# A chunked delta rule ahead of a mixture of experts on one core: keys of odd heads stored with the batches swapped

## The chip, the cores and the metric

The kernel runs on one core of a Trainium2 chip. It is one launch that computes everything. The time is the device time of an execution in microseconds; the figure for a kernel is the median of its runs. Five engines work side by side, each through its own queue in order: PE (matmuls, with the weight loads shown apart as PEld), DVE and ACT (elementwise work, both may read PSUM), POOL (elementwise work and indirect DMAs, no access to PSUM) and SP (DMA issues).

## The reference

Keys are normalised, then each head keeps a 48x48 state that every token reads and updates; the answers of all heads, side by side, are the 384 inputs of a router that sends each token to two of eight experts.

```
B, H, S, D = 4, 8, 768, 48        # N = B*S = 3072 tokens, E = 8, F = 1024
k_n = k / (norm(k, axis=-1, keepdims=True) + 1e-06)
for t in range(S):
    y[:, :, t] = einsum('bhd,bhde->bhe', q[:, :, t], state)
    v_old = einsum('bhde,bhd->bhe', state, kt)
    state = state + bt[..., None] * einsum('bhd,bhe->bhde', kt, vt - v_old)
x = y.transpose(0, 2, 1, 3).reshape(B * S, H * D)
noisy = x @ w_gate + log1p(exp(x @ w_noise)) * noise
# the two largest of each token, softmax over them, then
out[mask] += weight * (relu(x[mask] @ w1[e]) @ w2[e])
```

## The kernel before, in words

**Units and steps.** The sequence is cut into 12 chunks of 64 tokens (C = 64). A *unit* is one chunk of two batches, all 8 heads: partitions 0 to 63 hold the 64 tokens of one batch, 64 to 127 those of the other (`rows_of`). There are 2 units for a chunk (NU) and 24 in all; unit n belongs to chunk n // 2. Four units, two chunks, are a *step* (US = 4, six steps). Heads go in NP = 4 pairs j; z or y is the parity of a head within its pair, b the batch within the unit.

**What a unit does**, in the order of the data:

- `load` brings k, q and v of a unit, two DMAs for each (one per batch). SP issues them; ACT issues half of the k loads of the first step.
- `products`: PE turns k (`turned`, L549), ACT copies the turned keys to `kT` (L556), where rows 0 to 63 are the even head of a pair and 64 to 127 the odd one, and columns are the tokens of batch 0, then batch 1. `by_token` (L567) multiplies keys with keys, 32 matmuls of 64x64 over four 64-row tiles of the array. ACT (and DVE in the first step) copy the result to `gd` and `at`.
- Once per step DVE inverts 32x32 triangles of all four units at once: a transpose (L613), lengths of the keys (L641 to L652), 30 columns of two operations (L691, L695), two transposes back (L717, L725). These run at one instruction after another for some 30 us.
- `join` builds the inverse of 64x64 from the 32x32 pieces, with PE (L768, L774) and ACT (L748, L782, L786), into `w64`.
- `within`: PE turns q (L549), multiplies it with the keys (L567), DVE masks the result into `qk` (L810).
- `recur`: POOL scales v (L829); PE reads the old state with the keys (L567 with `st`), DVE subtracts (L848); PE multiplies with the inverse, the *solution* u (L858), ACT copies it (L865); PE sums keys times u (L876, the *state sum*) and DVE adds it to the state (L888, L892); POOL copies the new state into `wide` (L901), where each pair of heads has its two 48x48 states on a block diagonal of 128x96.
- `answer`: PE multiplies q with `wide` (L923, 16 matmuls, the *state answer*) and `qk` with u (L934, 32 matmuls, the *chunk answer*) into the same PSUM tile; ACT copies it to y (L959); PE turns y (L943), ACT copies (L965), PE multiplies with the router's weights (L948), ACT copies the logits (L973).

In the solution and the chunk answer every batch's 64 rows give results for the same 64 rows, so of the four 64-row tiles (row half times column half) they use (0, 0) and (1, 1).

**Routing and experts.** `route` chooses experts for one or two steps and POOL spreads their rows to DRAM by indirect DMA (L383). `early` computes part of expert 0 from rows of the first steps (L1256 to L1319). Everything from `rest` on (L1531 and others) belongs to the other experts and comes after the last step.

**Order.** `Jobs` holds every piece of the attention as a job with an engine, a planned cost and what it reads and writes, plans them greedily in time, and emits them in the planned order; each engine's queue keeps that order on the chip. PSUM is given out by the same plan: two single-bank tiles (`bank(1)`) and three two-bank tiles (`bank(2)`); jobs that may run ahead (`ahead=True`: key products, q-k products, the turns of k and q) use only the first single and the first two pairs. `opens` takes a tile from the plan, `closes` gives it back. Of those free, the one that has been empty longest is taken.

**Buffers.** Rings are indexed by unit: 12 slots for k, 10 for kT, 4 for q, v, qT, qk, and u, 2 per unit of a chunk for states and for `wide`. `early` reuses slots of k, kT and q.

Of the kernel before, what the change touches and what calls it, by code (L numbers as in the profile page):

```python
# [19 lines left out]
C = 64  # L20
DP = 64
# [211 lines left out]
def kernel(  # L233
# [39 lines left out]
    nc = tc.nc  # L273
# [7 lines left out]
    NU = B // 2  # L281
# [148 lines left out]
    def deltanet(ictx):  # L430
# [27 lines left out]
        def per_head(p):  # L458

            return p.tile[:, 0 : H * D].rearrange("p (h d) -> p h d", d=D)  # L460

# [4 lines left out]
        def by_parity(t):  # L466
            return t.rearrange("p (j z) d -> p z j d", z=2)

        NK, NT_, NW = 3 * US, 3 * US - NU, US + NU

        NQ, N_U, N_ST = 2 * NU, 2 * NU, 2
# [5 lines left out]

        wides = [
            ring(
                [128, 2, NP, 2 * D], f"wide{u}_", 2,  # L480
                lambda t: [t[0:DP, :, :, D:], t[DP:, :, :, 0:D]],
            )
            for u in range(NU)
        ]
# [22 lines left out]


# [15 lines left out]
        def load(n, name):  # L524
            c, u = divmod(n, NU)
            src, t, size = {"k": (k, kps, NK), "q": (q, qps, NQ), "v": (v, vs, NQ)}[name]
            for i, rows in enumerate(rows_of):
                engine = ACT if name == "k" and n < US and i else SP
                queue = nc.scalar if engine == ACT else nc.sync
# [9 lines left out]
        def halves(name, slot):  # L539
            return [(name, slot, i) for i in range(2)]  # L540
# [21 lines left out]
        def by_token(out, lhsT, rhs):  # L562

            for j in range(NP):
                for b in range(2):
                    for z in range(2):
                        nc.tensor.matmul(  # L567
                            out[rows_of[b], z, j], lhsT[rows_of[z], j, rows_of[b]],
                            rhs(rows_of[z], j, b), start=(j == 0), stop=(j == NP - 1),
                            skip_group_check=True,  # L570
                        )

        def products(n):
# [10 lines left out]
                    two_banks(p, C), kTs(n), lambda z, j, b: kTs(n)[z, j, rows_of[b]]  # L584
# [212 lines left out]
        def within(n):  # L797
# [6 lines left out]
                    two_banks(p, C), kTs(n), lambda z, j, b: qTs(n)[z, j, rows_of[b]]  # L804
# [12 lines left out]
        def recur(n):  # L817
# [4 lines left out]
            old, new, wide = sts[z](c), sts[z](c + 1), wides[z](c + 1)  # L822
            v_key, u_key = halves("v", n % NQ), ("u", n % N_U)
            every_w = [("w", n % NW), *(("w", n % NW, lo) for lo in range(0, 128, Q))]

# [10 lines left out]
            if c:  # L836
# [4 lines left out]
                        two_banks(p_b, D), kTs(n), lambda r, j, b: old[r, b, j]  # L841
# [11 lines left out]
            p_u = bank(1)  # L853

            def solve():
                for h in range(H):
                    for b in rows_of:
                        nc.tensor.matmul(  # L858
# [1026 lines left out]
```

## Time and profile before

| | |
|---|---|
| runs | 874.31, 875.14, 883.87 us; median 875.14 |
| profiled execution | 875.56 us; span from the first to the last instruction 873.8 us |
| instructions | 21991 |
| busy, share of the span | PE 772.6 us (88%), DVE 570.9 (65%), ACT 333.0 (38%), POOL 385.4 (44%) |
| first and last L613 (an inversion begins) | 17.1 and 228.0 us |
| last L725 (an inversion ends) | 298.2 us, 1.9 long |
| last logits multiplied (L948) | 358.6 us |
| DMA | 93.8 MB, mean 107 GB/s |

The profile is of one execution, taken on the chip; times in it count from the first instruction. Busy time of PE is modelled at the ends of matmuls. A group of instructions is written as line, engine, operation, output <- inputs, tile size of a matmul's stationary operand (rows*columns), shape of the output, count; then its busy time and the mean duration of one in ns, then the idle time of its engine just before and what ended it. "issue" stands for a wait for nothing that the profile shows. The granted PE clock is a share of the full clock: in this kernel it is 1.0 or 0.5 in each stretch of 3.4 us, and 0.89 in the mean.

### The profile page before, as it was taken

To read this page: it belongs to the slowest core of one execution; us is meant where nothing else is said; L and a number is where in the kernel's file an instruction comes from. 1 tells how busy PE (TensorE), PEld (TensorE's weight loads), DVE (VectorE), ACT (ScalarE), POOL (GpSimd) and SP (SyncE) were. 2 spreads that over 40 slices of the span, in tenths; PEclk is the share of its full clock that TensorE was granted. 3 is DMA by queue.
4 is the path that set the end of the run, shared out by engine and by line. 5 is a ranking of instruction groups with operands and counts; after the bars stand their busy time and mean duration, and the time that the engine had idled before them with its cause. 6 is when DMAs were issued, how large, how long until landed. Compare 5 with 4: busy or idle time off the path is not lost.

```text
span 873.8 us, 21991 instructions
## 1 busy us (share of the span) xinstructions
PE 772.6 (88%) x9110; PEld 602.7 (69%) x9110; DVE 570.9 (65%) x1295; ACT 333.0 (38%) x791; POOL 385.4 (44%) x424
## 2 busy tenths in 40 slices
PE   4657878887699786899999999999999999999995
PEld 3446767776588675646757858759668678588594
DVE  5987899989578542201579567677587496685651
ACT  4573667745354171311243053151251340531510
POOL 3021212021552544121268387477676674874511
PEclk8756878975597867899999999999999999999998
DMA  4789634624332313071272342524333421401101
GB/s 69 136 236 246 141 93 128 172 43 128 110 88 65 102 49 129 20 266 52 82 240 82 103 140 84 174 58 150 109 116 107 124 91 37 147 1 58 56 20 42
DMA packets 119087, 93.78 MB, mean 107 GB/s; under 512 B 84646, under 2 KB 109255, under 8 KB 118976
## 3 DMA queue, kind: packets, MB, share of 16 engines
q1 hardware_dynamic: 107312, 64.54, 26.7%
q0 software_dynamic: 9552, 27.33, 9.3%
q8 instruction: 74, 1.21, 0.6%
q10 hardware_dynamic: 2112, 0.39, 0.3%
q14 instruction: 37, 0.30, 0.1%
HBM read 58.82 MB, written 34.81 MB: 107 GB/s over the span
## 4 chain that ended last, share of the span: by engine, by line
PE 69%; issue 10%; DVE 9%; ACT 6%; POOL 3%; DMA 1%; another core or an unknown queue 1%; SPq 0%; POOLq 0%; DVEq 0%; ACTq 0%
PE inner L1531 24%; PE outer L1531 15%; PE pair L567 4%; PE pair L1282 3%; PE pair L1305 3%; PE single L858 3%; PE single L934 3%; DVE part L691 2%; DVE t L695 2%; PE single L549 2%; PE inner L1636 2%; PE inner L1563 2%; PE single L923 2%; PE single L948 1%; PE single L768 1%
## 5 line engine op out<-in xcount | busy, mean ns | idle before, releaser
L1590 DVE TENSOR_TENSOR hT<-hT,inner 128x416 f32<-128x416 f32 x182 | 105.5, 587 | 61.6 <-PE inner L1531 51.6
L1596 ACT ACTIVATE hT<-inner 128x416 f32<-128x416 f32 x112 | 57.9, 517 | 171.3 <-PE inner L1531 169.1
L424 POOL DMA_INDIRECT out_dram<-sums,index x49 | 50.8, 1037 | 113.7 <-DVE sums L1431 105.3
L1531 PE MATMUL inner<-s_x,w1e 128*128 128x416 f32 x196 | 78.7, 512 | 0.0
L1431 DVE SCALAR_TENSOR_TENSOR sums<-outer,gate,sums 128x192 f32<-128x192 f32 x112 | 45.1, 414 | 50.2 <-PE outer L1531 50.2
L901 POOL COPY wide<-st 64x384 f32<-64x384 f32 x44 | 24.8, 564 | 116.4 <-DVE st L888 94.7
L695 DVE TENSOR_TENSOR t<-t,part 128x30 f32<-128x30 f32 (+9 forms) x180 | 66.1, 367 | 6.2
L691 DVE TENSOR_TENSOR part<-t 128x30 f32<-128x30 f32 (+9 forms) x180 | 62.0, 345 | 5.0
L1585 ACT ACTIVATE hT<-hT 128x416 f32<-128x416 f32 x112 | 59.8, 547 | 12.2 <-DVE hT L1590 6.8
L1531 PE MATMUL outer<-t_w,hT 128*128 128x192 f32 x336 | 59.7, 328 | 0.0
L383 POOL DMA_INDIRECT rows_x<-y,slot x48 | 46.9, 977 | 27.3 <-issue 8.5
L1531 PEld LDWEIGHTS inner<-s_x,w1e 128*128 128x128 f32 x196 | 37.3, 190 | 31.2 <-issue 29.7
L415 POOL DMA_INDIRECT sums<-out_dram,index x49 | 52.6, 1073 | 13.8 <-issue 12.7
L1531 PE MATMUL inner<-xe,w1e 128*128 128x416 f32 x140 | 58.1, 513 | 0.0
L1531 PE MATMUL inner<-s_x,s_w 128*128 128x416 f32 x140 | 56.9, 512 | 0.0
L1531 PEld LDWEIGHTS outer<-t_w,hT 128*128 128x128 f32 x336 | 54.7, 190 | 0.4
L1568 ACT COPY xe<-inner 128x384 f32<-128x384 f32 (+1 forms) x49 | 20.1, 461 | 85.4 <-PE inner L1563 85.2
L1531 PE MATMUL outer<-w2e,hT 128*128 128x192 f32 x280 | 50.1, 326 | 0.0
L1531 PEld LDWEIGHTS outer<-w2e,hT 128*128 128x128 f32 x280 | 46.5, 190 | 2.2 <-issue 2.2
L1497 POOL TENSOR_TENSOR w1e<-w1e 128x256 f32<-128x256 f32 x54 | 46.3, 866 | 2.0
L660 POOL TENSOR_SCALAR_AFFINE_SELECT t<-t 128x1024 f32<-128x1024 f32 x6 | 7.6, 1269 | 86.2 <-DVE ss L631 39.6
L858 PE MATMUL single<-v,w 64*64 64x48 f32 x768 | 36.0, 255 | 9.1 <-issue 3.3
(222 smaller groups left out, 1707.2 us busy)
## 6 DMA issues: line engine op xcount, KB each, us to landing
w1e<-in_moe_w_dram SPq DMA_DIRECT2D x8, 1536.0 KB
w2e<-in_moe_w_dram SPq DMA_DIRECT2D x8, 1536.0 KB
xr<-rows_x SPq DMA_DIRECT2D x7, 1164.0 KB
rows_x<-empty SPq DMA_DIRECT2D x8, 776.0 KB
qp<-in_q_dram SPq DMA_DIRECT2D x48, 96.0 KB
v<-in_v_dram SPq DMA_DIRECT2D x48, 96.0 KB
out_dram<-empty SPq DMA_DIRECT2D x4, 1152.0 KB
kp<-in_k_dram SPq DMA_DIRECT2D x44, 96.0 KB
```

The source lines that it names most:

```text
L383: d = nc.gpsimd.indirect_dma_start(out=rows_x, out_offset=bass.IndirectOffsetOnAxis(ap=slot, axis=0), in_=rows, in_offset=None,).ins
L415: nc.gpsimd.indirect_dma_start(out=got, out_offset=None, in_=out, in_offset=bass.IndirectOffsetOnAxis(ap=index, axis=0), bounds_check=N - ...
L424: nc.gpsimd.indirect_dma_start(out=out, out_offset=bass.IndirectOffsetOnAxis(ap=index, axis=0), in_=got, in_offset=None, bounds_check=N - ...
L691: v_.tensor_tensor(out=part, in0=t[:, :, j + 1 :, j, None].to_broadcast(shape), in1=t[:, :, None, j, 0:j].to_broadcast(shape), op=ALU.mult,)
L695: v_.tensor_tensor(out=t[:, :, j + 1 :, 0:j], in0=t[:, :, j + 1 :, 0:j], in1=part, op=ALU.add)
L858: nc.tensor.matmul(per_head(p_u)[b, h], w64[b, h], v_n[b, h], start=(h == 0), stop=(h == H - 1), skip_group_check=True,)
L1431: nc.vector.scalar_tensor_tensor(out=got, in0=p, scalar=gate, in1=got, op0=ALU.mult, op1=ALU.add)
L1497: engine.tensor_tensor(out=block(to), in0=block(x), in1=block(y), op=ALU.add if sign == "+" else ALU.subtract,)
L1531: nc.tensor.matmul(p, lhsT, rhs, start=opens and i == 0, stop=i == len(products) - 1, skip_group_check=True,)
L1585: nc.scalar.activation(h, h, ACTF.Relu)
L1590: nc.vector.tensor_tensor(out=h, in0=h, in1=p, op=ALU.add if sign > 0 else ALU.subtract)
L1596: nc.scalar.mul(h, p, float(sign))
```

## The change

Keys of odd heads are loaded with the two batches swapped: rows 0 to 63 of the key tile hold batch 0 for even heads and batch 1 for odd ones. So `load` issues four DMAs for a unit's keys (batch by parity) instead of two, with a planned cost of 0.5 instead of 0.7. `crossed(z, b)` gives the half in which batch b of a head of parity z lies. u and `qk` follow the keys' layout; v, the inverse, q and y keep theirs. Solution and chunk answer so take rows of one half to columns of the other for odd heads, and write two-bank PSUM tiles, one bank per parity. The state answer is read straight from the state, with 32 matmuls of 48 columns, as a job of its own ahead of the solution; `wide` and its POOL copies are gone. kT gets 12 slots instead of 10; q, v, qT and qk 6 instead of 4.

```diff
-        NK, NT_, NW = 3 * US, 3 * US - NU, US + NU
-
-        NQ, N_U, N_ST = 2 * NU, 2 * NU, 2
+        NK, NT_, NW = 3 * US, 3 * US, US + NU
+
+        NQ, N_U, N_ST = 3 * NU, 2 * NU, 2
...
-        wides = [
-            ring(
-                [128, 2, NP, 2 * D], f"wide{u}_", 2,
-                lambda t: [t[0:DP, :, :, D:], t[DP:, :, :, 0:D]],
-            )
-            for u in range(NU)
-        ]
         vs = ring([128, H, D], "v", NQ)
...
+        def crossed(z, b):
+
+            return rows_of[b ^ z]
...
+            if name == "k":
+                for i in range(2):
+                    for z in range(2):
+                        engine = ACT if n < US and i else SP
+                        queue = nc.scalar if engine == ACT else nc.sync
+                        jobs.add(
+                            engine, 0.5,
+                            lambda i=i, z=z, queue=queue: queue.dma_start(
+                                out=t(n)[rows_of[i]][:, z::2, 0:D],
+                                in_=src[2 * u + (i ^ z), z::2, c * C : (c + 1) * C].rearrange(
+                                    "h p d -> p h d"
+                                ),
+                            ),
+                            writes=[(name, n % size, i, z)], lands=2.0, moves=0.35,
+                        )
+                return
...
-        def by_token(out, lhsT, rhs):
+        def by_token(out, to, kT, rhs):
 
             for j in range(NP):
                 for b in range(2):
                     for z in range(2):
                         nc.tensor.matmul(
-                            out[rows_of[b], z, j], lhsT[rows_of[z], j, rows_of[b]],
-                            rhs(rows_of[z], j, b), start=(j == 0), stop=(j == NP - 1),
+                            out[to(z, b), z, j], kT[rows_of[z], j, crossed(z, b)],
+                            rhs(z, j, b), start=(j == 0), stop=(j == NP - 1),
                             skip_group_check=True,
                         )
+
+        def straight(z, b):
+            return rows_of[b]
...
-                    two_banks(p, C), kTs(n), lambda z, j, b: qTs(n)[z, j, rows_of[b]]
+                    two_banks(p, C), crossed, kTs(n),
+                    lambda z, j, b: qTs(n)[rows_of[z], j, rows_of[b]],
...
+            p_y, qT = bank(2), qTs(n)
+
+            def of_state():
+                for j in range(NP):
+                    for b in range(2):
+                        for y in range(2):
+                            nc.tensor.matmul(
+                                two_banks(p_y, D)[rows_of[b], y, j],
+                                qT[rows_of[y], j, rows_of[b]], old[rows_of[y], b, j],
+                                start=(j == 0), stop=False, skip_group_check=True,
...
+                    PE, 0.55, of_state,
+                    reads=[("qT", n % NQ), ("qk", n % NQ), ("st", z, c % N_ST)],
+                    writes=[("of_state", z)], opens=p_y,
+                )
+            p_u = bank(2)
             def solve():
-                for h in range(H):
-                    for b in rows_of:
-                        nc.tensor.matmul(
-                            per_head(p_u)[b, h], w64[b, h], v_n[b, h],
-                            start=(h == 0), stop=(h == H - 1), skip_group_check=True,
-                        )
-
-            jobs.add(PE, 1.1, solve, reads=[*v_key, *every_w], opens=p_u)
-            jobs.add(
-                ACT, 0.5, lambda: nc.scalar.copy(u_n, per_head(p_u)),
+                for j in range(NP):
+                    for b in range(2):
+                        for y in range(2):
+                            nc.tensor.matmul(
+                                two_banks(p_u, D)[crossed(y, b), y, j],
+                                w64[rows_of[b], 2 * j + y], v_n[rows_of[b], 2 * j + y],
+                                start=(j == 0), stop=(j == NP - 1), skip_group_check=True,
+                            )
+
+            jobs.add(
+                PE, 0.55, solve, reads=[*v_key, *every_w, *([("of_state", z)] if c else [])],
+                opens=p_u,
+            )
+            jobs.add(
+                ACT, 0.5, lambda: nc.scalar.copy(by_parity(u_n), two_banks(p_u, D)),
                 writes=[u_key], closes=p_u,
...
-                                kp[rows_of[b], 2 * j + y], u_n[rows_of[b], 2 * j + y],
+                                kp[crossed(y, b), 2 * j + y], u_n[crossed(y, b), 2 * j + y],
...
-            def widen():
-                return [
-                    nc.gpsimd.tensor_copy(wide[rows, :, :, y * D : (y + 1) * D], new[rows])
-                    for y, rows in enumerate(rows_of)
-                ]
-
-            jobs.add(
-                POOL, 1.25, widen, reads=[("st", z, (c + 1) % N_ST)],
-                writes=[("wide", z, (c + 1) % 2)],
-            )
-
-        def answer(n):
+            return p_y
...
-            def of_state():
+            def of_chunk():
                 for j in range(NP):
-                    for b in rows_of:
-                        nc.tensor.matmul(
-                            per_head(p_y)[b, 2 * j : 2 * j + 2], qT[:, j, b],
-                            wide[:, b.start // C, j],
-                            start=(j == 0), stop=False, skip_group_check=True,
-                        )
-
-            def of_chunk():
-                if c:
-                    of_state()
-                for h in range(H):
-                    for b in rows_of:
-                        nc.tensor.matmul(
-                            per_head(p_y)[b, h], qk[b, h % 2, h // 2], u_n[b, h],
-                            start=(c == 0 and h == 0), stop=(h == H - 1),
-                            skip_group_check=True,
-                        )
+                    for b in range(2):
+                        for y in range(2):
+                            nc.tensor.matmul(
+                                two_banks(p_y, D)[rows_of[b], y, j],
+                                qk[crossed(y, b), y, j], u_n[crossed(y, b), 2 * j + y],
+                                start=(c == 0 and j == 0), stop=(j == NP - 1),
+                                skip_group_check=True,
+                            )
...
-                reads.append(("wide", z, c % 2))
-            jobs.add(PE, 1.9 if c else 1.0, of_chunk, reads=reads, opens=p_y)
+                reads.append(("of_state", z))
+            jobs.add(PE, 0.6, of_chunk, reads=reads, **{"uses" if c else "opens": p_y})
             jobs.add(
                 ACT, 0.5,
-                lambda: nc.scalar.copy(y_n, per_head(p_y).rearrange("p h d -> p (h d)")),
+                lambda: nc.scalar.copy(
+                    y_n.rearrange("p (j z d) -> p z j d", z=2, d=D), two_banks(p_y, D)
+                ),
                 writes=[y_key], closes=p_y,
...
-                recur(n)
-                answer(n)
+                answer(n, recur(n))
```

## The prediction

> **What bounds the kernel now.** I read first the busy time by stretch, with cuts at the DVE transposes that begin the inversions (L613) and at the last one that ends one (L725, done at 300.1 us). The columns are stretch, length, busy time of each engine with its instructions, granted PE clock, DMA share, GB/s.
>
> ```profile
> 17.10:228.00 210.90, 159.20 (x4118) 137.47 (x4118) 184.10 (x454) 126.93 (x327) 36.73 (x51) 0.73 0.59 144
> 228.00:300.10 72.10, 61.26 (x1591) 55.02 (x1595) 50.95 (x134) 26.39 (x69) 32.91 (x43) 0.79 0.32 86
> 300.10:366.10 66.00, 49.06 (x1002) 41.55 (x1003) 19.59 (x85) 26.51 (x77) 23.80 (x29) 0.79 0.21 74
> 366.10:420.00 53.90, 53.38 (x180) 30.34 (x179) 4.35 (x17) 7.60 (x19) 11.65 (x12) 0.97 0.39 136
> 420.00:873.80 453.80, 441.85 (x2081) 332.29 (x2081) 302.71 (x559) 138.15 (x283) 273.29 (x257) 0.99 0.30 97
> ```
>
> Three regimes. From 17 to 228 us DVE, with five inversions end to end, is busy 87% and PE 75%: DVE sets the pace. In the sixth inversion (228 to 300) PE is busy 85% and DVE 71%: PE sets it. In the tail (300 to 366) PE does the last recurrences at 74%, with waits. From 366 on PE is 98% busy with the experts, which the diff does not touch; it moves forward or back with the tail.
>
> Then the groups of instructions up to 366 us, for the steps that the diff rewrites (busy, mean ns of one, idle before).
>
> ```profile
> L858 PE MATMUL single<-v,w 64*64 64x48 f32 x768 | 36.0, 255 | 9.1 <-issue 3.3 <-ACT w L786 3.3 <-ACT u L865 2.4
> L934 PE MATMUL single<-u,qk 64*64 64x48 f32 x768 | 34.5, 243 | 5.0 <-issue 5.0
> L923 PE MATMUL single<-wide,qT 128*64 128x96 f32 x352 | 23.8, 287 | 5.3 <-ACT w L786 2.6 <-ACT logits L973 2.2 <-POOL wide L901 0.2
> L876 PE MATMUL pair<-u,kp 64*64 64x48 f32 x704 | 17.8, 247 | 2.7 <-issue 2.0 <-ACT u L865 0.5
> L901 POOL COPY wide<-st 64x384 f32<-64x384 f32 x44 | 24.8, 564 | 116.4 <-DVE st L888 94.7 <-DVE st L892 13.7 <-DMA rows_x<-y,slot 7.0
> ```
>
> L858 (solution) and L934 (answer) use two of the four 64-row tiles, 1.50 and 1.44 us busy per unit (36.0/24, 34.5/24). L876 issues as many matmuls of the same shape over all four, 0.81 us (17.8/22). Last, the timeline, at the start and in the tail.
>
> ```profile
> 0.84 3.57 ACTq L532 DMA_DIRECT2D kp<-in_k_dram  x4
> 5.67 0.58 ACT L556 COPY kT<-single 128x512 f32<-128x512 f32 x1 [3.58 <-PE single L549]
> ...
> 343.11 0.96 POOL L383 DMA_INDIRECT rows_x<-y,slot  x1 [0.30 <-issue]
> 343.61 0.25 PEld L934 LDWEIGHTS single<-u,qk 64*64 64x64 f32 x5 [1.20 <-issue]
> 343.61 0.36 PE L934 MATMUL single<-u,qk 64*64 64x48 f32 x5 [0.51 <-issue]
> 344.37 0.96 POOL L383 DMA_INDIRECT rows_x<-y,slot  x1 [0.30 <-issue]
> ```
>
> At the start ACT issues k loads and then copies kT. In the tail, while POOL's row spreads (L383) follow one another every 1.26 us, PE waits for nothing that is shown and gets 3 to 5 matmuls in that time: one chunk answer lasts from 342.2 to 350.3. The same happens at 227 to 236, 290 to 293 and 301 to 309, always from the second or third spread of a run on.
>
> **The change part by part.** First the price of a unit on PE, from start to next start where PE has no gap. Four-tile L876 takes 0.61 us at the full clock and 1.02 at half. Solution: 0.86 and 1.53. Answer from the chunk: 1.06 and 1.54. Answer from the state (16 matmuls of 96 columns): 0.81 and 1.48. With all three at L876's price a unit saves 0.25+0.45+0.20 = 0.9 us at full clock, 0.51+0.52+0.46 = 1.5 at half: some 28 us over 24 units. What arrives at the end differs by stretch.
>
> *Start, +2.3.* ACT issues 4 k loads in 3.57 us, 0.89 each; now 8, done at 0.84+7.14 = 7.98. The planner puts them ahead of the first kT copy (their planned 8x0.5 = 4.0 us end before the copy's planned start), so that copy moves from 5.67 to 7.98, and with it gd and the first inversion. Bounds: 0 (copy goes between) and +3.6.
>
> *17 to 228 us, -4.8.* PE's saving hides under DVE. Exceptions: DVE waits for PE 5.9 us between 71 and 91 (L892, L848, L810); three half-clock solves and answers there give 1.5. And DVE operations of the inversion (L691, L695) that overlap a widening copy run some 0.18 us longer than the fastest of their shape; I added these excesses: 3.8 us here, 1.7 after 228. At 87% DVE share: 3.3.
>
> *228 to 300 us, -7.0.* In it lie 7 solutions (5 at full clock), 8 chunk answers and 8 state answers (5 each): 5x0.25+2x0.51 = 2.3; 5x0.45+3x0.52 = 3.8; 5x0.20+3x0.46 = 2.4; 8.5 together, at PE's 85% share 7.0 to 7.2; I take 7.0. The 1.7 us of DVE excess I count as covered by PE (0 to 1.7). That the widening is no longer waited for is worth little: PE shows 0.2 us of it in all (L923).
>
> *Tail, -8.7.* Four solutions 1.8, four chunk answers 1.9, four state answers 1.1: 4.7 with rounding. With six q buffers the four q turns (3.7 us of PE) and four q-k products (3.2) of the last step need not wait for the step before and can leave the tail, for a stretch that is 85% full: 0 to 6.9; I take 4, as PE there gains the 8.5.
>
> *Costs elsewhere, +5.* SP issues 40 more k loads at 0.63 = 25 us, mostly while it waits for buffers; in the first 48 us its queue has no gap, q and v loads stand behind the k loads, and k of units 8 to 11 would land at about 47 instead of 33 where PE wants the last at 44.3: 0 to +5, I take 1. PSUM: the state's answer now opens a two-bank tile before the solution and holds it until the answer is copied, and the solution takes another; there are three. 0 to +28 (the second rival), I take 3. The clock: the granted clock was 0.63 from 187 to 228 us, where PE was 72% busy, 0.82 from 140 to 187, where it was 90%; less work may mean a slower clock: 0 to +4, I take 1. The solution also waits newly for the state's answer, thus for the q-k product: nothing, as long as that comes a step early. kT with 12 slots instead of 10 frees the products of units 22 and 23 from the wait for L567 of units 12 and 13 (206 and 217 us): DVE is busy until 227.9 anyway, so nothing.
>
> *The spreads, 0.* Their number stays; POOL loses the 44 widening copies that stand between some of them. Bounds: -12 (runs broken up) and +13 (the first rival).
>
> Sum: 2.3-4.8-7.0-8.7+5 = -13.2. The profiled execution took 875.6 us (span 873.8 and 1.8 around it), 0.4 over the median of 875.14: 862 in either reading.
>
> In the new solution, chunk answer and state sum both row halves of the array write each PSUM bank, which L876 does not do today. Do four tiles still work side by side? The joins L768 and L774 do it with four row groups and one bank: their 64 matmuls begin at 191.42 and the next work at 192.10, 10.6 ns each. So I take yes; if not, the solutions' and chunk answers' gains go (5.2 in the sixth inversion, 3.7 in the tail, 1.5 before) and the state sum loses (10 units after 228 at 0.4): 10.4+4 = 14.4, and the sum is +1.2. A rule of the Trainium skill, TensorEngine Tiling (Array Packing), section Gotcha 1: PSUM Pressure, says just that, that different row tiles cannot access one PSUM bank at the same time; by it the time would be 877.
>
> **Rivals.** (1) *PE's gain does not arrive*, 875 us, within 1%. Without the widening copies, which wait for DVE between the spreads (at 245 to 267 and 292 to 298), more spreads run back to back and PE gets 3 to 5 matmuls for each. Today some 18 of the 40 spreads before 366 us starve it; of two routes of 16, 28 could: 10 to 16 more at 1.26 us, less what DVE hides, 13: 862+13 = 875. The tiles' failing to overlap (+14.4) ends at the same place. Against it: the v products (L829) still stand between spreads, and the joins speak for overlap. (2) *Two-bank tiles run out*, 887 us, the slower side. The state's answer for the next step's first two units is ready as soon as L567 reads their state (90.8 us for units 4 and 5); their answers came at 122.9 to 127. If both held tiles are pairs 0 and 1, products of keys, which may use only these, stand still that long. For the last inversion: units 12 and 13 would hold from 206 and 217 to 246, products of units 20 to 23 (211 to 224) would follow at 246 to 256, 28 us late; DVE's slack in that stretch takes few of them: 862-3+28 = 887. It decides once both pairs are held while products are pending; the extra kT slots, which let products go before, speak against it. (3) *The tail closes up*, 844 us: step 5's joins begin at 310.7 though its inverse was ready at 300.1, as PE, starved by spreads, still had answers of step 4 to do. If these are out of the way by 300, some 10 us more; the rest of the moved q work 2.9, the costs of clock, start and pairs less 5: 862-18 = 844.
>
> **How the numbers follow.** Forecast (847 to 866) 0.52, rival 3 0.06, rival 1 0.22, rival 2 0.20. Predicted time 862. About 1% (8.8 us) is what a measurement of this kernel can tell from no change: faster is 0.52+0.06 = 0.58, same 0.22, slower 0.20. For the range I leave out rival 3 and the upper half of rival 2, 0.16: 846 to 887; the forecast's own is 847 to 866.
>
> **What would show it.** Solution and answers at about 0.6 us of PE per unit at full clock and 1.0 at half; the first L613 near 19.4; no widening copy, and DVE's L691 and L695 closer to their fastest; a sixth inversion of some 65 us instead of 72; the q turns of the last step before 300; the expert work beginning near 353 instead of 366 and as long as before. I am wrong if the four-tile steps stay over 0.8 us at full clock, if L613 of the sixth inversion comes after 235 with products of keys just before it, if chunk answers spread out over more spreads than now, or if the time from 300 on does not shrink.

## The result, and the profile after

The changed kernel takes 885.48 us (median of 20 runs, 874.46 to 891.1) where the kernel before, run beside it, takes 874.96: a ratio of 1.0098, 95% interval 1.0069 to 1.0126. In a second comparison it was 1.0149 (1.0087 to 1.0211). The forecast was 862, and faster; the time came out near where the second rival had put it (887). Ratios leave out executions more than 1.5% above the fastest of their kernel. The profiled execution took 881.57 us, its span is 879.8. Timelines below show chosen lines in order of time.

Busy time by stretch of the changed kernel, cut at the same events as before (first and last begin of an inversion, now L626, at 19.2 and 249.7 us; the last inversion's end at 323.7; the first dense expert matmul at 375.0). Columns: stretch, length, busy time of each engine with its instructions, granted PE clock, DMA share, GB/s.

```profile
19.20:249.70 230.50, 155.54 (x4282) 131.43 (x4282) 176.16 (x453) 127.60 (x330) 34.91 (x39) 0.69 0.59 146
249.70:323.70 74.00, 59.83 (x1937) 53.27 (x1936) 52.10 (x144) 30.17 (x80) 17.12 (x20) 0.74 0.20 57
323.70:375.00 51.30, 37.87 (x850) 32.33 (x843) 21.38 (x88) 21.52 (x63) 19.61 (x23) 0.60 0.22 76
375.00:430.00 55.00, 53.40 (x194) 31.59 (x193) 6.23 (x18) 8.49 (x22) 11.24 (x11) 1.00 0.37 130
```

The first stretch was 210.9 us long and is 230.5, with DVE busy 76% of it instead of 87%. The sixth inversion is no shorter (72.1 before, 74.0 now). The tail is 15 us shorter, but starts 24 us later. The experts begin 8 us late and then take 504.8 us to the end (506.9 before).

The groups of instructions on PE up to 375 us (busy, mean ns of one, idle before):

```profile
L890 PE MATMUL pair<-v,w 64*64 64x48 f32 x768 | 24.1, 284 | 7.5 <-DVE v L874 5.9 <-issue 1.5
L949 PE MATMUL pair<-u,qk 64*64 64x48 f32 x768 | 23.2, 280 | 5.5 <-ACT u L901 4.9 <-issue 0.6
L845 PE MATMUL pair<-st,qT 64*64 64x48 f32 x704 | 19.4, 273 | 4.9 <-DVE v L874 4.0 <-DVE qk L824 0.5 <-ACT at L615 0.4
```

Solution, chunk answer and state's answer are busy 66.7 us; they were 94.3 (36.0, 34.5 and 23.8). From start to next start a solution now takes 0.58 us at the full clock and 1.00 at half, a chunk answer 0.58 and 0.89, a state's answer 0.57 and 0.89. The new thing in these lines is "DVE v L874": 4.1 of its 5.9 us are a wait of a solution for DVE to read something else out of PSUM.

One place where time went is unit 10. In the kernel before its solution began at 182.1 us, 2.2 us after its v was ready (L848). In the changed one it began at 212.1. The kernel before, with the key product of unit 23 as the last line:

```profile
179.30 0.55 DVE L848 TENSOR_TENSOR v<-v,pair 128x384 f32<-128x384 f32 x1
182.10 1.83 PE L858 MATMUL single<-v,w 64*64 64x48 f32 x29
223.40 1.13 PE L567 MATMUL pair<-kT 64*64 64x64 f32 x32 [0.94 <-ACT at L602]
```

The changed kernel around unit 10:

```profile
197.22 1.10 PE L576 MATMUL pair<-st,kT 64*64 64x48 f32 x32
200.21 1.96 PE L845 MATMUL pair<-st,qT 64*64 64x48 f32 x64
...
211.36 0.55 DVE L874 TENSOR_TENSOR v<-v,pair 128x384 f32<-128x384 f32 x1
212.05 1.10 PE L890 MATMUL pair<-v,w 64*64 64x48 f32 x32 [4.11 <-DVE v L874]
```

At 197 us the state is read with the keys of unit 11 into one two-bank tile, at 200 the state's answers of units 10 and 11 open the other two. The v of unit 10 was ready by then, at 195.65 (179.85 before), so 15.8 of the 30 us were lost ahead of this scene. Its solution still waits for a tile: two are held until the chunk answers, which need the solutions, and the third until DVE subtracts for unit 11, which stands in DVE's queue behind the key lengths of the fifth inversion (DVE waited 4.3 us for ACT's root there) and eleven of its columns. At 211.9 DVE is through and 0.1 us later the solution starts. Before, the solution took a single-bank tile.

Then the delay runs on. K loads of units 22 and 23 need the state sums of units 10 and 11, and their products come late, into a run of row spreads:

```profile
234.85 0.34 PE L781 MATMUL single<-tb,at 32*32 32x32 f32 x5 [1.18 <-issue]
236.84 0.48 PE L576 MATMUL pair<-kT 64*64 64x64 f32 x3 [1.03 <-ACT at L615]
240.66 0.48 PE L576 MATMUL pair<-kT 64*64 64x64 f32 x4 [0.94 <-issue]
244.40 0.34 PE L576 MATMUL pair<-kT 64*64 64x64 f32 x1 [0.28 <-issue]
```

The L576 lines are some of the 32 matmuls of unit 23's key product, spread from 236.8 to 244.7 us (223.4 us was its start before). The sixth inversion needs them. DVE's group of the two transposes that begin the fifth and the sixth inversion, between 186 and 251 us, before (L613) and now (L626):

```profile
L613 DVE STREAM_TRANSPOSE t<-gd 128x1024 f32<-128x1024 f32 x2 | 3.9, 1928 | 0.1
L626 DVE STREAM_TRANSPOSE t<-gd 128x1024 f32<-128x1024 f32 x2 | 3.9, 1934 | 16.0 <-ACT gd L609 16.0
```

DVE was idle 16.0 us ahead of one of them; in the kernel before it was 0.1. The fifth interval between inversions grew from 41.3 to 57.4 us, and in the second profile of the changed kernel it was 57.3: so it is no accident of one run.

### The profile page after: what moved, and what is told of

It is laid out like the page before. It is cut to its first block, busy times and chain, and to the rows that moved or that the text cites. A ratio compares the mean times of both kernels' runs of the same rounds, so it can differ in the third digit from the quotient of the medians.

```text
span 879.8 us, 22711 instructions
## 1 busy us (share of the span) xinstructions
PE 753.7 (86%) x9462; PEld 584.6 (66%) x9462; DVE 564.0 (64%) x1297; ACT 332.4 (38%) x791; POOL 357.0 (41%) x372
## 4 chain that ended last, share of the span: by engine, by line
PE 61%; DVE 13%; issue 7%; ACT 5%; SPq 5%; another core or an unknown queue 4%; POOL 2%; DMA 2%; POOLq 0%; DVEq 0%; ACTq 0%
PE inner L1548 24%; PE outer L1548 14%; DVE part L704 3%; DVE t L708 3%; PE pair L1300 3%; PE pair L1323 3%; PE inner L1653 2%; PE inner L1580 2%; SPq L526 2%; SPq L377 2%; PE pair L890 1%; PE pair L949 1%; PE single L558 1%; PE pair L576 1%
## 5 line engine op out<-in xcount | busy, mean ns | idle before, releaser
L708 DVE TENSOR_TENSOR t<-t,part 128x30 f32<-128x30 f32 (+9 forms) x180 | 61.1, 339 | 6.2
L704 DVE TENSOR_TENSOR part<-t 128x30 f32<-128x30 f32 (+9 forms) x180 | 60.2, 334 | 5.1
L558 PE MATMUL single<-ident,kp 128*128 128x128 f32 x96 | 22.7, 380 | 23.7 <-DMA kp<-in_k_dram 14.7
L1548 PEld LDWEIGHTS inner<-s_x,s_w 128*128 128x128 f32 x140 | 26.6, 190 | 22.3 <-issue 22.3
```

What stands on the lines that cost most here:

```text
L558: nc.tensor.transpose(p_t[:, j], src(n)[:, 2 * j : 2 * j + 2], ident)
L704: v_.tensor_tensor(out=part, in0=t[:, :, j + 1 :, j, None].to_broadcast(shape), in1=t[:, :, None, j, 0:j].to_broadcast(shape), op=ALU.mult,)
L708: v_.tensor_tensor(out=t[:, :, j + 1 :, 0:j], in0=t[:, :, j + 1 :, 0:j], in1=part, op=ALU.add)
L1548: nc.tensor.matmul(p, lhsT, rhs, start=opens and i == 0, stop=i == len(products) - 1, skip_group_check=True,)
```

## The experiments

The times of "before" differ by chip: 875 to 879 us in most comparisons, 847 in two of them (late_state to order_only, share_answer to after_other_order), the difference ahead of the expert work, since from its first matmul to the end all kernels of the table but more_k take 504 to 509 us on either kind of chip. Ratios are against the kernel before in the same rounds. Edits are shown shortened to the lines that carry them.

The expectations call the theories by letters. A: two-bank tiles run out. B: the k loads wait in SP's queue or for their slots. C: the planner's order is luck. D: the larger rings hurt. E: the widening copies are missing between the spreads. F: PE's time is hidden behind DVE's queue.

The table holds what I worked out from each trace. "Experts" is the first dense expert matmul. PE busy and idle are up to there. "Held" is the time in which all three two-bank tiles are held, each from the first matmul that opens it to the end of the instruction that reads it last; the last column is PE's idle time inside that time. These two columns say where PE is idle, not what it waits for.

| kernel | ratio (95%) | experts, us | PE busy | PE idle | held | idle in it |
|---|---|---|---|---|---|---|
| before_again | 1 | 366.5 | 281 | 85 | 57 | 9 |
| other_order | 0.996 (0.992 to 1.000) | 369.2 | 283 | 86 | 48 | 11 |
| twice | 1.043 (1.037 to 1.050) | 408.5 | 323 | 85 | 37 | 9 |
| keep_widening | 0.995 (0.989 to 1.001) | 372.6 | 272 | 101 | 83 | 29 |
| after_again | 1.015 (1.009 to 1.021) | 381.6 | 268 | 113 | 124 | 42 |
| keep_early | 1.017 (1.003 to 1.030) | 388.7 | 283 | 106 | 145 | 52 |
| old_rings | 1.025 (1.015 to 1.036) | 387.7 | 276 | 112 | 134 | 46 |
| late_reserve | 1.014 (1.003 to 1.025) | 375.9 | 261 | 115 | 126 | 34 |
| one_tile_late | 1.009 (1.006 to 1.013) | 378.2 | 259 | 120 | 133 | 52 |
| *the quicker chip:* order_only | 1.011 (1.003 to 1.020) | 348.9 | 270 | 79 | 64 | 20 |
| four_loads | 1.010 (1.003 to 1.018) | 347.1 | 270 | 77 | 72 | 18 |
| keep_other_order | 1.011 (1.003 to 1.019) | 346.8 | 257 | 90 | 98 | 32 |
| late_state | 1.013 (1.005 to 1.021) | 349.8 | 255 | 95 | 98 | 29 |
| after_other_order | 1.014 (1.005 to 1.022) | 353.8 | 254 | 100 | 126 | 43 |
| more_k | 1.028 (1.021 to 1.036) | 348.5 | 257 | 91 | 137 | 40 |

**late_state.** The job of the state's answer waits for what the solution waits for:

```
- reads=[("qT", n % NQ), ("qk", n % NQ), ("st", z, c % N_ST)], writes=[("of_state", z)]
+ reads=[("qT", n % NQ), ("qk", n % NQ), *v_key, *every_w], writes=[("of_state", z)]
```

> The changed kernel with one edit: the state's answer is opened only when the scaled v and the inverse are there (just ahead of the solution) instead of as soon as q and the state are. Theory A (two-bank tiles run out, because state's answers hold them for long): the solution of unit 10, issued at 212 us in the changed kernel, comes back to about 190, the fifth inversion interval shrinks from 57 us to about 45, and the time falls to about 870 us. Theory B (the k loads wait in SP's queue behind v loads and for old slots, whatever the tiles do): unit 10 moves little, the last key products stay at 230 to 240 us, the time stays at 880 to 888. Theory C (the planner's order alone is luck): no size is given by it, the interval that is long would be another one.

1.013. The fifth interval shrank to 38 us, as theory A wanted, but unit 10's solution came at 208.6 and not at 190. The timeline around it:

```profile
194.83 1.10 PE L576 MATMUL pair<-qT,kT 64*64 64x64 f32 x32
199.61 1.96 PE L845 MATMUL pair<-st,qT 64*64 64x48 f32 x64 [0.50 <-DVE v L874]
207.78 0.68 DVE L824 TENSOR_TENSOR qk<-pair,mask 128x512 f32<-128x512 f32 x1
208.62 1.10 PE L890 MATMUL pair<-v,w 64*64 64x48 f32 x32 [3.00 <-DVE qk L824]
```

The two answers of the chunk again hold two tiles, and the third is a q-k product whose mask DVE applies 12 us later. The holder changed, the wait stayed. Theory A's size failed; the wait it names is in the trace.

**more_k.**

```
- NK, NT_, NW = 3 * US, 3 * US, US + NU
+ NK, NT_, NW = 4 * US, 3 * US, US + NU
- NQ, N_U, N_ST = 3 * NU, 2 * NU, 2
+ NQ, N_U, N_ST = 2 * NU, 2 * NU, 2
```

> The changed kernel with 16 slots for k instead of 12, and 4 for q instead of 6, so that a k load of the last step needs the state sum of unit 6 or 7 and no longer that of unit 10 or 11. Theory B (k loads are held by their slots): the last key products come before 225 us instead of 237 to 245, the fifth interval is 45 us or less, and the time is about 870 us. Theory A (two-bank tiles): the solution of unit 10 stays late (after 205 us), products wait for a pair, and the time stays at 880 or above.

1.028 (1.021 to 1.036). Theory B's first half holds: the last key product came at 207.2 us, the fifth interval was 41.5. The time did not follow. The experts began at 348.5, with late_state and order_only; 15.2 us more were lost at 400 us, where PE waited for the rows of the rest ("DMA xr<-rows_x"), a place that no theory had named. Unit 10's solution stayed late (210.8). So here more slots for k brought the keys earlier and not the end of the attention. All three tiles were held 137 us, twice the 64 of order_only, and yet the experts began at the same time in both: the time held is no price.

**four_loads.** The kernel before with the four k loads of the changed kernel, straight instead of crossed.

```
- out=t(n)[rows][:, :, 0:D], in_=src[2 * u + i, :, c * C : (c + 1) * C]
+ for z in range(2): out=t(n)[rows_of[i]][:, z::2, 0:D], in_=src[2 * u + i, z::2, c * C : (c + 1) * C]
```

> The kernel before with k brought by four DMAs of a parity each instead of two, and nothing else. Theory A: only the start is later, by the 2.1 us of the first inversion, 877 us. Theory B: SP's and ACT's queues cost more than that and the key products come late in the later steps too: 880 us or more, with PE's turns waiting for k 14 us instead of 9. Theory C (luck of the order): a change of either sign up to 9 us.

1.010. The first inversion came at 19.2 us, as in the changed kernel. PE's idle (77) is near that of order_only (79) on the same chip, but its waits for loads of k and q in the first 53 us came to 15.8 us instead of 9.6. The last key product came at 238.5 us (222.1 in order_only) and the fifth interval was 51.1 (39.1), with the solution in its single bank. So late keys and a long fifth interval come without the pressure on the tiles too, and here they did not hold back the experts (347.1 against 348.9). The 1% cannot be told from what any new order does, as the next two show.

**order_only and other_order.** The work of before in two other orders: planned costs in the one, patience in the other.

```
- jobs.add(PE, 1.1, solve, ...)      jobs.add(PE, 1.9 if c else 1.0, of_chunk, ...)
+ jobs.add(PE, 0.55, solve, ...)     jobs.add(PE, 1.15 if c else 0.6, of_chunk, ...)
```

```
- PATIENCE = 0.05
+ PATIENCE = 0.1
```

> The kernel before with the planned costs alone changed: 0.55 instead of 1.1 for a solution, 1.15 instead of 1.9 for an answer; the same instructions in another order. Theory C (the planner's order decides, and costs planned below the measured ones hurt): 880 to 890 us. Theories A and B: within 4 us of before, 871 to 879.

> The kernel before with one constant of the planner changed, patience 0.1 instead of 0.05 us, so that nothing but the order in the queues differs. Theory C: 1.005 to 1.015, as with order_only (1.011); if 0.995 to 1.004, the order before is not special and what the changed kernels lose is theirs.

1.011 and 0.996. An order alone is worth half a per cent down or one up. The order before is not the best there is, so luck alone does not explain the changed kernels; but differences of one per cent between two single kernels must not be read as a cause.

**before_again and after_again.** Both kernels unchanged, on one chip.

> The kernel before, unchanged, for a trace on the same chip as the kernels beside it. The time before the first dense expert matmul (366.9 us in the first profile) is expected shorter where the runs of spreads are shorter; from there to the end 507 us as before.

> The changed kernel, unchanged, timed in the same rounds as the kernels beside it. All theories: about 1 per cent slower than before (1.010). If on this chip too the fifth interval between inversions is near 57 us, it is the order of the queues that makes it; if it is below 45, the wait seen first was an accident of the spreads.

Busy times from 0 to the expert work (columns as in the first view), of before_again, after_again, and the kernel twice, which comes next:

```profile
0.00:366.50 366.50, 281.24 (x6852) 242.67 (x6853) 264.75 (x729) 187.84 (x489) 101.17 (x155) 0.75 0.46 115
```

```profile
0.00:381.50 381.50, 268.08 (x7204) 227.40 (x7205) 259.27 (x731) 186.92 (x489) 76.85 (x107) 0.69 0.45 113
```

```profile
0.00:408.50 408.50, 323.20 (x8388) 281.97 (x8389) 262.71 (x729) 188.71 (x489) 101.17 (x155) 0.81 0.41 104
```

From the first to the second PE is busy 13.2 us less and idle 28.2 us more (85.3, then 113.4). PE's idle time where all three two-bank tiles are held grew by 33 us (42 against 9), and elsewhere it fell by 5; they are all held 124 us instead of 57. What PE waits for is more mixed. Waits up to the experts that a reader of some other two-bank tile ended came to 9.1 us, then 18.8. Waits for loads of k and q came to 9.3, then 18.8, most of it in the first 50 us. Waits with no cause shown came to 28.0, then 38.5. So some 10 of the 28 us are seen to be waits for a tile.

**twice.** Every matmul of the solution and of the chunk answer is issued two times; the planned costs, and so all queues, stay as before.

```
- for h in range(H):                  # solve
+ for h in [*range(H), *range(H)]:
...                                    # the chunk answer: a second loop ahead of the first
```

> The kernel before with every matmul of the solutions and of the chunk answers issued twice (the second pass overwrites the first), the planner told the same costs, so that all queues keep the order of before and PE alone gets some 50 us more work (48 jobs of 0.86 to 1.54 us). It measures what PE's time in just the steps that the change shortens is worth with nothing else moved. If they lie on the path that sets the end, as the prediction had it for the stretches behind the fifth inversion, at least half of it arrives: 1.03 to 1.055. If the recurrence waits for DVE's queue and PE's time there is mostly hidden (theory F), less than a quarter arrives: 1.00 to 1.015.

1.043. In the third line above PE is busy 42.0 us more and idle 85.3 us, as in the kernel before (on another chip, where before takes 879). The experts begin 42 us later and the medians differ by 37 (916.0 and 879.4), so PE time added to these steps arrives almost in full; theory F falls. So the prediction was right to count PE's time. That saved time would arrive as fully, had the waits not grown, is likely but not shown.

**keep_widening.** The changed kernel, but the state's answer is taken from the widened state inside the answer's job, so that its tile is opened after the solution; rings of before.

```
- jobs.add(PE, 0.55, of_state, ..., writes=[("of_state", z)], opens=p_y)
...
- two_banks(p_y, D)[rows_of[b], y, j], qT[rows_of[y], j, rows_of[b]], old[rows_of[y], b, j]
+ two_banks(p_y, D)[rows_of[b], y, j], qT[:, j, rows_of[b]], wide[:, b, j, y * D : (y + 1) * D]
...
- jobs.add(PE, 0.6, of_chunk, reads=reads, **{"uses" if c else "opens": p_y})
+ jobs.add(PE, 1.4 if c else 0.6, of_chunk, reads=reads, opens=p_y)   # of_state, then the chunk
```

> The changed kernel with the widening kept: crossed keys, solution and chunk answer over four tiles, the state's answer from the widened state by 32 matmuls of 48 columns inside the answer's job, so that its two-bank tile is opened late; rings of before. Theory A: unit 10's solution is back near 190 us, fifth interval 45 us or less, 0.985 to 0.995 of before. Theory C: 1.005 to 1.015 whatever the tiles do. Theory B (k loads in four): 1.005 to 1.01.

0.995. Unit 10's solution came at 192.7, as soon as v was there:

```profile
192.03 0.51 DVE L868 TENSOR_TENSOR v<-v,pair 128x384 f32<-128x384 f32 x1
192.71 1.90 PE L879 MATMUL pair<-v,w 64*64 64x48 f32 x64
```

The fifth interval was 50.7 us in this profile, not 45. All three tiles are held 83 us instead of 124. The ten runs spread from 868.1 to 885.5 us, and their plain median, 879.3, lies above the 875.6 of before, so the gain is not certain.

**keep_other_order.** The same with another patience:

```
- PATIENCE = 0.05
+ PATIENCE = 0.1
```

> The kernel keep_widening with the planner's patience 0.1 instead of 0.05 us: the same work in another order, to see how much of 0.995 is the luck of one order. Theory A: 0.98 to 1.005. If it is above 1.01, the order in the queues weighs as much as the tile does.

keep_widening in this second order came out at 1.011: the gain of the first does not stand by itself.

**keep_early.** keep_widening with the opening moved back: the state's answer in a job of its own ahead of the solution, which now also waits for it.

```
+ jobs.add(PE, 0.8, of_state, reads=[..., ("wide", z, c % 2)], writes=[("of_state", z)], opens=p_y)
- solve: reads=[*v_key, *every_w]
+ solve: reads=[*v_key, *every_w, ("of_state", z)]
```

> The kernel keep_widening (crossed keys, state widened, rings of before) with one thing put back: the answer's two-bank tile is opened ahead of the solution, by a job of its own, as in the changed kernel. Theory A (two tiles held across the solution): the gain of keep_widening (0.995) goes, 1.005 to 1.02, and in the trace a solution of unit 8 to 12 waits 8 to 16 us for a tile that DVE has not read yet. Theory E (it is the missing widening copies, which keep POOL and so the spreads apart): it stays at 0.99 to 1.00.

1.017; the intervals of the two, each beside before on its own chip, do not overlap. Units 10 and 11 repeat the changed kernel's scene:

```profile
196.88 1.10 PE L583 MATMUL pair<-st,kT 64*64 64x48 f32 x32 [2.57 <-DVE qk L831]
199.72 1.96 PE L852 MATMUL pair<-wide,qT 128*64 128x48 f32 x32 [0.73 <-DVE norms L694]
210.49 0.55 DVE L880 TENSOR_TENSOR v<-v,pair 128x384 f32<-128x384 f32 x1
211.09 1.10 PE L896 MATMUL pair<-v,w 64*64 64x48 f32 x32 [0.79 <-DVE v L880]
```

The widening copies are all there, so theory E falls: it is not their absence. PE's waits that a reader of another two-bank tile ended rose from 9 to 24 us. PE's idle time within "all held" rose from 29 to 52 us. It fell elsewhere, so that idle in all grew by 5 only; the other 11 us of the 16 to the experts are PE busy longer, at a granted clock of 0.67 instead of 0.72.

**no_widen.** The kernel before without the widening: state's answer from the state over four tiles, opened just ahead of the solution, which stays in a single bank.

```
- jobs.add(POOL, 1.25, widen, ...)
+ jobs.add(PE, 0.55, of_state, reads=[..., *v_key, *every_w], writes=[("of_state", z)], opens=p_y)
```

> The kernel before with the widening alone taken away: keys, solution and chunk answer stay as they were (two tiles, keys not crossed), the state's answer is read from the state over four tiles into a two-bank tile, opened just ahead of the solution. It leaves out the crossing. Theory A (the widening's removal is good by itself, the early hold of tiles is what costs): 0.985 to 0.995 of before, with no wait of a solution for a tile. Theory C (any other order of the queues costs about a per cent, since the order before is a lucky one): 1.005 to 1.015.

1.007 (1.002 to 1.011). Removing the widening alone gains nothing in this form either.

**old_rings.**

```
- NK, NT_, NW = 3 * US, 3 * US, US + NU
+ NK, NT_, NW = 3 * US, 3 * US - NU, US + NU
- NQ, N_U, N_ST = 3 * NU, 2 * NU, 2
+ NQ, N_U, N_ST = 2 * NU, 2 * NU, 2
```

> The changed kernel with the ring sizes of before (10 slots for kT and at, 4 for q, v, qT and qk). Theory A (tiles: every solution now needs a two-bank tile, and the two answers of the chunk that were opened ahead of it hold two of the three): as the changed kernel, 1.010 to 1.020 of before, unit 10's solution after 205 us or another solution as late behind a tile. Theory D (the larger rings are what keep_widening leaves out and what hurts): 0.99 to 1.00.

1.025 against 1.015 with them (on two chips): the larger rings are not what hurts, theory D falls.

**late_reserve.** late_state, and:

```
- p_y = bank(2)
+ p_y = bank(2, True)
```

> The changed kernel with the state's answer opened late, just ahead of its solution, and its tile taken from pairs 0 and 1 alone, as products are, so that pair 2 only ever serves the recurrence. Theory A: unit 10's solution no longer waits for a q-k product's tile (208.6 us with the late opening alone), it starts within 3 us of its state's answer, and the ratio falls from 1.013 to 1.000 or below. The rival in the prediction (products blocked by answers held in pairs 0 and 1): key products of the last step come after 235 us and the ratio is 1.01 to 1.03. Theory C (order luck): 1.005 to 1.015.

1.014. At unit 10 theory A's wait went, and the rival's late keys came: unit 10's solution started 0.9 us after its state's answer, and the sixth inversion began at 262.7 us, later than in any kernel but two of the table. Units 10 and 23:

```profile
201.81 1.11 PE L845 MATMUL pair<-st,qT 64*64 64x48 f32 x32 [0.68 <-DVE v L874]
202.70 1.07 PE L890 MATMUL pair<-v,w 64*64 64x48 f32 x32
...
256.00 1.10 PE L558 MATMUL single<-ident,kp 128*128 128x128 f32 x4
259.22 0.69 PE L576 MATMUL pair<-kT 64*64 64x64 f32 x32
```

Unit 23's keys stood in PE's queue behind the solution of unit 13, which began at 253.2. Sparing one user of the three tiles here delayed another.

**share_answer, share_late, one_tile_late.** The answers of a chunk's two units lie side by side in one two-bank tile (192 of 512 columns each), in the second and third opened late as in late_state. In share_answer and share_late the copy of the first unit's answer is not tied behind its chunk answer, so that part of y is not the reference's.

```
+ cols = slice(z * NP * D, (z + 1) * NP * D)        # unit z of the chunk
- solve reads ("of_state", z)
+ solve reads ("of_state", 0), ("of_state", 1)
```

> The changed kernel with the state's answers of a chunk's two units put side by side into one two-bank tile (192 columns of each bank for each unit; both state's answers stand ahead of the first solution), so that two answers held across the solutions take one tile of three instead of two. Theory A (two-bank tiles held across the solution): the solution of unit 10 starts within 5 us of its state's answer (11.8 us in the changed kernel on this chip), the key products of the last step come before 230 us, and the ratio falls from 1.015 to 0.985 to 0.998. Theory E (POOL's missing copies) or the loads of k: it stays at 1.010 to 1.020.

> The same shared tile, with the state's answers opened only when the scaled v and the inverse of their unit are there. Theory A: the tile is held for a shorter time, but the first unit's solution now waits for the second unit's v as well: 0.985 to 1.005, within 1 per cent of the shared tile opened early. If the early opening is a cost of its own beside the number of tiles, this one is faster by 1 per cent or more.

> share_late with the copy of the first unit's answer ordered behind its chunk answer, which share_answer and share_late had left free to come too early. Theory A: about the time of share_late (1.005) or less: 0.99 to 1.008, so 1 per cent below the changed kernel; if the missing order had bought time, 1.008 to 1.015.

1.011 (1.004 to 1.019), 1.005 (1.001 to 1.009) and, with the order mended, 1.009. Unit 10's solution started 2.8, 2.8 and 7.7 us after its state's answer, but in none did the ratio fall below 1. Theory A in its narrow form, that the second held tile is the whole cost, fails: in one_tile_late all three tiles are still held for 133 us. Its fifth interval is 75.3 us. There a unit's solution waits for the other unit's v too (unit 12: state's answer at 234.8, that of unit 13 at 247.3, solution at 250.7), so it is likely that the shared order takes what the tile gives.

**after_other_order.** The changed kernel with the patience of keep_other_order.

> The changed kernel with the planner's patience 0.1 instead of 0.05 us. Theory A: a solution of one of the units 8 to 13 again waits 7 us or more for a tile, and the ratio is 1.005 to 1.02. Theory C (luck of the order): anything, below 1.00 too.

1.014, unit 10's solution 12 us behind its state's answer again (204.5 and 216.6). The loss came in both orders tried.

## Why the prediction was wrong

*Unit prices: right.* 0.61 us and 1.02 were taken for a four-tile step, 0.57 to 0.58 and 0.89 to 1.00 came. In the solution and the chunk answer two row halves of the array now write each bank, in the state's answer one does, and at the full clock all take the same time. The rule that the prediction weighed (the Trainium skill, TensorEngine Tiling (Array Packing), Gotcha 1: PSUM Pressure) is that different row tiles cannot access one PSUM bank at the same time. No price of it shows in this trace, and the measurement decides; whether two row halves ever wrote one bank at the same moment it does not tell.

*By stretch.* The profiled execution was 2.1 us later at the first inversion, 19.6 longer from there to the last one's begin, 1.9 longer in the sixth inversion, 14.7 shorter in the tail and 2.9 shorter after it: 6.0 longer in all, where 13.2 less had been forecast. The miss lies mostly ahead of the sixth inversion.

*Start, +2.3: right.* ACT issues its eight loads in 6.54 us and copies the first kT at 7.42; the first inversion moved by 2.1 us, from 17.1 to 19.2.

*The 28 us on PE: mis-sized, 13.* Busy time to the experts fell by 13.2 us on one chip (17.2 in the first pair of profiles). Of the 306 jobs of the attention on PE, 151 started at the half clock instead of 121; 30 jobs at some 0.4 us more (1.02 less 0.61) are 12 us, which is most of what is missing. The "clock, +1" was this term, and by this estimate it was some ten times as large.

*17 to 228 us, -4.8: right in its term, and lost.* DVE's columns ran faster without the widening copies (L691 and L695 128.1 us, L704 and L708 121.3; 5.5 was predicted in all). But the stretch ended 21.7 us later. That PE's time there hides under DVE is not borne out: the work added in twice moved the begin of the last inversion from 228.1 to 248.1 us (on another chip).

*Sixth inversion, -7.0; tail, -8.7.* The first did not come (74.0 us against 72.1). The tail shrank by 15 us in the first profile and by 4 in the second (66.7 to 63.1); the last q turn did leave it, as forecast, and ended at 285 us instead of 338. Neither carried the experts forward.

*PSUM pairs, +3: the step that failed.* The prediction counted the solution as a new user of a two-bank tile and priced that at 3 us, without asking who would hold the other two when it is due. The state's answers of its chunk hold them, until the chunk answers, which need the solutions. So the first job to stand still was the solution, which before had a single bank: at unit 10 it began 11.8 us behind its state's answer, in both profiles. The last inversion began 21.7 and 19.6 us later than before, and PE's idle time to the experts grew by 28.2 us against the 13.2 us saved. About 10 of the 28.2 are seen to be waits for a tile, about as many are waits for loads; what the tiles cost in all stays open. The second rival named this shortage, with key products standing still because answers hold pairs 0 and 1; the first job to stand still was another. That 28 was also its bound is chance, since it meant the begin of the last inversion, and so in part is its 887: it added 28 to gains of which some did not come.

*The spreads, 0; rival 1.* The key product of unit 23 did fall into a run of spreads, because it was late. With the widening copies back (keep_early) the loss stayed, so the missing copies are not what made it.

*What stays open.* Shown are that PE time added to these steps arrives almost in full (twice), that the changed kernel's solution of unit 10 waits for a tile in two orders (after_again and after_other_order), and that the kernel which opens the answer early is slower than the one which opens it late: 1.017 against 0.995 of before, 1.021 against 1.004 by plain medians (keep_early and keep_widening). Not shown is how much of that is the planner's order, since one kernel in two orders differed by 1.6% (keep_widening and keep_other_order). The changed kernel's own loss, 1.0 and 1.5%, is of the same size, so the share of the tiles in it stays open too. The fifth interval does not settle it: late_state has 38.2 us and loses 1.3%, four_loads has 51.1 and loses 1.0%. A kernel with the change and without the added pressure on the pairs was not run. No version tried beats the kernel before beyond doubt; keep_widening and other_order come nearest, at 0.995 and 0.996.

## What to carry to other kernels

When an edit moves a job from one pool of PSUM tiles to another, list for each tile who holds it, until which instruction on which engine, and whether that instruction waits for the job itself; an accumulator opened ahead of the step that must fill it takes its tile away for that whole wait. Count the time in which all tiles of a pool are held, before and after: here it doubled, and PE's idle time grew by a third. That shows where to look and is no price: of the 28 us more, some 10 were waits that a reader of another tile ended. Where a planner orders the queues, measure two or three orders of the same work first, to know what one per cent means; here an order alone moved the time by 0.4% down and 1.1% up.

## What the hardware showed unexpectedly

With more work on PE the rest of its work took less time. In twice, solutions and chunk answers are busy 126.5 us instead of 71.3, 55 us more, yet PE's busy time grew by 42.0: the granted clock up to the experts was 0.81 instead of 0.75, and 95 of 354 jobs began at half clock instead of 121 of 306 (on two chips). The changed kernel went the other way, to 0.69.

Chips differ ahead of the experts and hardly behind them: order_only, with the instructions of before in another order, began the experts at 348.9 us where before_again and other_order on slower chips began at 366.5 and 369.2, and then took 505.5 us to the end against 506.1 and 506.2.
